# Turning u by a transposing transfer instead of TensorE and ScalarE, with a schedule of nine sets of ranks, in a fused threshold-attention and mixer kernel

## The chip, the cores and the metric

The kernel runs on one core of one Trainium2 chip. Its time is the device time of one execution in microseconds. The number quoted for the kernel before is the median of three runs. The profile is that of one further execution.

## What is computed

Eight batches of eight attention heads (sequence 576, head size 64) go through an attention that keeps only scores close to each row's largest one. The result, laid out as 576 rows of 512 channels for each batch, then goes through a mixer: a low-rank mixing along the sequence and a two-layer perceptron with a residual.

```python
# attention: batch, heads, seq, head_dim = 8, 8, 576, 64
scores = scale * np.matmul(q, k.transpose(0, 1, 3, 2))
thresh = np.max(scores, axis=-1, keepdims=True) - tau
scores = np.where(scores >= thresh, scores, -1000000000.0)
scores = scores - np.max(scores, axis=-1, keepdims=True)
attn = np.exp(scores)
attn = attn / (np.sum(attn, axis=-1, keepdims=True) + 1e-09)
x = np.matmul(attn, v)                    # then heads side by side: 8 x 576 x 512
# mixer: rank 32, d_model 512, hidden 2048
xt = x.transpose(0, 2, 1)
h = xt @ U @ V
u = x + h.transpose(0, 2, 1)
ch = np.maximum(u @ w_ch1, 0.0) @ w_ch2
out = u + ch
```

The first layer of the perceptron contracts over the 512 channels. TensorE contracts over the partitions, so the kernel needs u with the channels on the partitions, that is, u turned. That turning is what the change touches.

## The kernel before

The kernel works through 32 pairs of heads (four for each batch), and has its own small list scheduler. Each piece of work is a task with an engine, a cost, the tasks that it depends on, and a function that emits the instructions. The scheduler simulates the five engines with those costs, and emits the tasks in the order that it finds. Each engine then executes its instructions strictly in that fixed order. Where several tasks of one engine could start, a rank decides: the time at which the task became ready, plus an offset for its kind of task. The offsets stand in a table with one column for each phase of the program.

```python
OFF = {
    "copy_main": (-65.55, 4.27, -33.19), "copy_rest": (46.32, -22.93, -32.89), ...
    # ... one entry for each kind of task, three numbers each
}
def add(self, *args, **kw):
    t = Task(*args, **kw)
    t.off = self.OFF[t.fn.__name__][self.phase]
# ...
def rank(c):
    s, t = c
    if t.when is not None:
        due = t.when <= steps + (1.0 if t.kind == kind else 0.0)
        return (t.when - 1000.0 if due else t.when + 1000000.0, s)
    return (t.ready + t.off, s)
```

A matmul group of the perceptron carries a `when`, counted in score steps. It goes first once that many score steps have been emitted, and otherwise it takes the place that nothing else wants. There are 144 score steps in all; `DUE` holds the number for each batch.

```python
DUE = (218.25, 193.25, 202, 58.75, 370.75, 342.5, 322.25, 741.75)
# ...
if e == PE:
    n = free[0]
    while at[PE] + 0.45 < s and last[n] <= at[PE]:
        self.filler(n)               # a matmul on the identity that nothing reads
```

The softmax of one score step (128 rows of two heads), cut: TensorE makes scores in PSUM, VectorE takes them out with their minimum, ScalarE makes the exponential, VectorE selects. GpSimd doubles a part of the result, and SyncE's transposing transfer turns the weights.

```python
nc.tensor.matmul(pair_bank[j][part, c, 0:HC], a.tT[hs, 0, rows], a.tT[hs, 1, cs], ...)   # L449
nc.vector.tensor_scalar(out=s_sb, in0=pair_bank[x][:, :, 0:HC], ...)                     # L462
nc.scalar.activation(out=e_sb, in_=s_sb, func=ACT.Exp, ...)                              # L482
nc.vector.scalar_tensor_tensor(out=w_sb[:, 0:S], in0=s_sb, ..., in1=e_sb, ...)           # L489
nc.gpsimd.tensor_copy(out=w_sb[:, xs, S:640], in_=w_sb[:, xs, 512:S])                    # L507
nc.sync.dma_start_transpose(to, w_ring[...])                                             # L513
```

What follows for a head pair (cut): the product with the values (L588 to L596), the low-rank product (L653), its spread (L668), the sum u, its narrowing to bf16, and the turning of u.

```python
def sum_u(_):                                                        # VectorE, L675
    nc.vector.tensor_add(out=bt.x[:, :, pr.cols], in0=bank[...], in1=bt.x[:, :, pr.cols])

def narrow_u(_):                                                     # ScalarE, L682
    nc.scalar.copy(out=pr.ub, in_=bt.x[:, :, pr.cols])

ub = done["ub", p] = add(SCA, 0.57, narrow_u, [u, got("uT_", p - 2), got("ub", p - 1)])

def turn_u(t):                                                       # TensorE, L690
    ps = bank[t.got[0]][:, 0:256].bitcast(BF16)
    for i in range(4):
        nc.tensor.transpose(ps[:, i * P:(i + 1) * P], pr.ub[:, i, :], identb)

uT_ = done["uT_", p] = add(PE, 0.23, turn_u, deps, banks=1, kind="uT")

def copy_u(_):                                                       # ScalarE, L696
    nc.scalar.copy(out=bt.uT[:, pr.hp, :], in_=bank[uT_.got[0]][:, 0:256].bitcast(BF16))
```

The perceptron of a batch reads `bt.uT` in its first layer, ScalarE applies the relu (L750), the second layer follows, and VectorE adds u (L805).

```python
nc.tensor.matmul(bank[t.got[0]], W1b[:, dt, ft * P:(ft + 1) * P], bt.uT[:, dt, :], ...)  # L760, "up"
nc.tensor.matmul(ch, R2[:, ft, lo:lo + P], W2b[:, ft, :], ...)                           # L793, "down"
```

The 64 rows of each batch that are left over beyond 512 are gathered over two batches. They are turned on TensorE (L727) and go through the first layer at L776.

Of the kernel before, what the change touches and what calls it, by code (L numbers as in the profile page):

```python
# [8 lines left out]
P = 128  # L9
FP32 = mybir.dt.float32  # L10
BF16 = mybir.dt.bfloat16
# [11 lines left out]
NPAIR = H // 2  # L23
NP = B * NPAIR
SOFT = 4
EARLY = 8


W1_AT = (1, 4, 6, 9, 11, 14, 16, 19)
W2_AT = (20, 21, 23, 24, 25, 26, 28, 29)  # L30

DUE = (218.25, 193.25, 202, 58.75, 370.75, 342.5, 322.25, 741.75)

# [11 lines left out]
PE, VEC, SCA, POOL, SP = range(5)  # L45
# [19 lines left out]
class Order:  # L65
# [12 lines left out]


    OFF = {  # L80
        "copy_main": (-65.55, 4.27, -33.19), "copy_rest": (46.32, -22.93, -32.89), "copy_tt":
        (55.52, 75.97, 78.39), "copy_u": (-9.24, 32.51, 27.95), "copy_u4": (-33.7, -103.34, 12.57),
        "copy_w": (26.76, -36.81, 20.04), "down": (9.11, -38.52, 30.41), "exponential": (-75.1,
        348.03, 34.33), "finish": (-81.29, -4.31, -38.11), "first": (-55.84, 39.98, -12.2), "high":
        (318.07, 5.62, 10.21), "inverse": (-108.97, -22.9, -67.36), "join": (10.42, -3.6, 8.15),
        "load": (-8.71, 35.51, -42.16), "low": (12.45, 36.07, 40.66), "low_part": (-39.21, 135.95,
        -5.41), "low_rank": (-33.23, -18.24, 8.92), "make": (-24.27, 38.39, 1.66), "narrow": (-16.4,
        -76.48, 195.67), "narrow_u": (60.65, 3.75, -17.1), "narrow_u4": (-18.43, 20.09, 16.7),
        "norm": (-28.14, -232.63, 8.05), "product": (124.81, 96.76, 14.8), "relu": (108.49, 92.35,
        46.18), "rest": (63.06, -59.16, 27.83), "scores": (-50.96, -12.67, -95.71), "select":  # L90
        (118.77, 57.08, 91.87), "send": (-69.4, 60.79, -21.09), "spread": (48.74, -2.19, -63.39),
        "spread4": (79.29, 25.05, 4.44), "spread_v": (11.62, 75.45, 21.95), "sum_u": (-26.95,
        -36.59, 53.52), "sum_u4": (54.92, -47.81, 31.47), "sums": (-140.25, 32.72, -84.66),
        "threshold": (-37.93, 79.1, -43.59), "turn4": (71.1, 12.6, 27.31), "turn_main": (-113.51,
        69.4, 58.93), "turn_pe": (-18.8, -21.2, 34.54), "turn_rest": (15.16, 27.93, 15.36),
        "turn_u": (-21.99, 92.75, -1.81), "turn_w": (-17.93, -115.14, 3.52), "twin": (-84.09,
        -15.28, -93.69), "up": (-7.21, -32.4, -1.5), "values": (-8.3, -68.34, -10.67), "weigh":
        (28.1, 41.88, 60.36), "weights": (8.1, -7.95, 22.31),
    }

    def __init__(self, nbanks, filler):
# [5 lines left out]
        self.tasks.append(t)  # L107
        return t
# [90 lines left out]
def kernel(  # L199
# [12 lines left out]
    nc = tc.nc  # L212
# [10 lines left out]
    identb = consts.tile([P, P], BF16, name="identb")  # L223
# [59 lines left out]
    bank = [psum.tile([P, 512], FP32, name=f"bank{n}") for n in range(4)]  # L283
# [8 lines left out]
    order = Order(len(bank), fill)  # L292
    add = order.add

    done = {}

    def got(*key):
        return done.get(key)
# [72 lines left out]
            pairs.append(Pair(b, hp, batches[-1]))  # L371


    def prepare_tasks(p):
        pr = pairs[p]
        loads = load_tasks(p, pr)
        before = [got("S", p - 2, 3), got("S", p - 2, 4)]
        for x, (name, t0) in enumerate((("q", 0), ("k", 5))):
            def turn_main(t, t0=t0):
                for i in range(4):  # L380
                    nc.tensor.transpose(bank[t.got[0]][:, i * P:(i + 1) * P],  # L381
                                        pr.qkraw[:, t0 + i, :, :], ident)
# [24 lines left out]

        def high(_):
            nc.scalar.copy(out=pr.vh[:, :, :, 0, :],  # L409
                           in_=pr.vraw.rearrange("p j t d -> p t j d"))  # L410

        def low(_):

            raw = pr.vraw.rearrange("p j t d -> p t j d")
            for part, tiles_, h in ((slice(0, P), slice(0, 4), 1), (slice(HB, P), slice(4, 5), 0)):
                nc.gpsimd.tensor_tensor(out=pr.vh[part, tiles_, :, h, :], in0=raw[part, tiles_],  # L416
                                        in1=pr.vh[part, tiles_, :, 0, :], op=ALU.subtract)

        t = done["vhi", p] = add(SCA, 0.7, high,
                                 loads["v"] + [got("AV", p - 2, g) for g in range(3)] + [got("vhi", p - 1)])  # L420
        done["vlo", p] = add(POOL, 1.6, low, [t])
# [4 lines left out]
    gate = {}  # L426

    def score_tasks(p, i):


        pr = pairs[p]
        n = step[0]
# [5 lines left out]
        def scores(_):  # L438

            for c in range(2):  # L440
# [11 lines left out]
        deps = [got(name, p + a) for a in range(2 if i == 4 else 1)  # L452
                for name in ("qT", "kT", "qk4T")]
# [6 lines left out]
        for x in range(2):  # L460
# [6 lines left out]
            t = add(VEC, 0.69, weigh, [S_, got("w", tiles[0] + x - NS)])  # L467
# [12 lines left out]
        for x in range(2):  # L480
# [44 lines left out]
            if i < 4 and (x == 1 and p < EARLY and i >= 1 or p == NPAIR - 1 and i == 3):  # L525
                t = done["wT", tiles[0]] = add(PE, 0.28, turn_pe, [twin_] + free, banks=1,
                                               kind="wT")
# [18 lines left out]
        if i == 4:  # L546

            def sums(_):
# [3 lines left out]
                                        dma=0.1)  # L552


    def value_tasks(p):
        pr = pairs[p]
        bt = pr.batch

# [13 lines left out]
        for g, tiles_ in enumerate(((0, 1), (2, 3), (4,))):  # L572
            n = len(tiles_)
# [39 lines left out]
            if soft:  # L613
                def make(_, rows=rows, over_sum=over_sum, av=av, n=n):
# [5 lines left out]
                              frees=[av]))  # L620
# [14 lines left out]
            t = add(SCA, 0.36 if n == 2 else 0.28, low_part, [av] + opens)  # L635
            t = add(VEC, 0.35 if n == 2 else 0.22, join, [t], frees=[av])
# [46 lines left out]

        ub = done["ub", p] = add(SCA, 0.57, narrow_u, [u, got("uT_", p - 2), got("ub", p - 1)])

        def turn_u(t):

            ps = bank[t.got[0]][:, 0:256].bitcast(BF16)
            for i in range(4):
                nc.tensor.transpose(ps[:, i * P:(i + 1) * P], pr.ub[:, i, :], identb)  # L690

        deps = [ub] + (done.get(("p1", pr.b - 2), []) if pr.hp == 0 else [])
        uT_ = done["uT_", p] = add(PE, 0.23, turn_u, deps, banks=1, kind="uT")

        def copy_u(_):
            nc.scalar.copy(out=bt.uT[:, pr.hp, :], in_=bank[uT_.got[0]][:, 0:256].bitcast(BF16))  # L696

        done["uT", p] = add(SCA, 0.53, copy_u, [uT_, got("uT", p - 1)], frees=[uT_])


        if not last:
            return
# [1 line left out]
        def spread4(t):  # L704
# [4 lines left out]
                                    banks=1, kind="h")  # L709
# [29 lines left out]
    ov = out.rearrange("b (p t) m -> b p t m", p=HB)  # L739

    def mixer_tasks(b):
        bt = batches[b]

        due = DUE[b]
        uT = [done["uT", b * NPAIR + hp] for hp in range(NPAIR)]
# [11 lines left out]
        for ft in range(16):  # L757
            def up(t, ft=ft):
                for dt in range(4):
# [3 lines left out]
            t = add(PE, 0.862, up, uT + weights1 + done.get(("o", b - 2), []), banks=1, kind="p1",  # L763
                    when=due + 35.75 * ft / 16)
# [3 lines left out]
        if bt.odd:  # L768

            done["p1r", b] = []  # L770
            for g in range(4):
                def rest(t, g=g):
                    for n in range(4):
# [6 lines left out]
                t = add(PE, 0.9, rest, [done["uT4", b], got("o4", b - 2)] + weights1, banks=1,  # L780
                        kind="p1", when=due + 3.5 + 10.25 * g)
# [94 lines left out]

    weight_loads()
    for p in range(0, NP, 2):
        order.phase = 0 if p < NPAIR else 1 if p < NP - NPAIR else 2
        prepare_tasks(p)  # L880
        prepare_tasks(p + 1)
        for i in range(NT):
            score_tasks(p, i)
        for i in range(4):
            score_tasks(p + 1, i)
        value_tasks(p)
        value_tasks(p + 1)
        if (p + 1) % NPAIR == NPAIR - 1:
            mixer_tasks(p // NPAIR)
# [37 lines left out]
```

## Time and profile before

| what | value |
|---|---|
| time, median of three runs | 615.9 us (615.58 to 616.2) |
| span of the profiled execution | 612.9 us |
| granted TensorE clock | 0.999 of full speed |
| DMA traffic | 87.35 MB, mean 143 GB/s |
| the transposes of u on TensorE (L690) | 128 instructions, 219 ns each |
| the copies of the turned u on ScalarE (L696) | 32 instructions, 579 ns each |
| the transposing transfers of the weights (L513) | 143, median 4.5 us from issue to landing |

The profile gives each engine's busy time, and groups instructions by the kernel's line. A busy TensorE is not necessarily a TensorE at its peak, because matmuls overlap in its pipeline: the durations of neighbouring matmuls add up to more than the time that they took together. For that reason the distance between the starts of neighbouring matmuls is used here wherever TensorE's work is counted.

### The profile page before, as it was taken

Reading aid. Unit: us, or ns where it says so; the run is one execution under the profiler, and the core shown is the slowest. Engines: PE = TensorE matmul, PEld = TensorE weight load, DVE = VectorE, ACT = ScalarE, POOL = GpSimd, SP = SyncE. Lnnn points to the kernel's source line nnn. Section 1 sums busy time; section 2 is a strip of 40 time slices with the busy share of each in tenths; the row PEclk is TensorE's granted clock in tenths of the full one; section 3 lists DMA queues with packets and bytes.
Section 4 is the critical chain, followed back from the end, with each engine's and each line's share of the span. In section 5 each row is a group of like instructions: output and inputs, shape, how many; then the busy total and the mean of one; then the engine's idle time right before and its main releaser. Section 6 shows DMA issues by size and latency. Waiting matters only on the chain.

```text
span 612.9 us, 17317 instructions
## 1 busy us (share of the span) xinstructions
PE 600.8 (98%) x6339; PEld 346.1 (56%) x6339; DVE 521.0 (85%) x1399; ACT 478.3 (78%) x983; POOL 361.2 (59%) x596
## 2 busy tenths in 40 slices
PE   7999999999999999999999999999999999999997
PEld 4465655656556555655456655564656655555553
DVE  3999998899999899899976999999998899994201
ACT  4778899988898867997687966998789877984540
POOL 8787768687887656556535755676675732442000
PEclk9999999999999999999999999999999999999999
DMA  7699989987999699977994799889867896464203
GB/s 158 124 167 150 170 152 155 149 157 152 185 163 160 147 174 155 176 146 153 177 157 89 127 182 158 163 135 169 164 129 135 160 196 115 88 126 87 65 13 73
DMA packets 209716, 87.35 MB, mean 143 GB/s; under 512 B 187744, under 2 KB 199984, under 8 KB 209632
## 3 DMA queue, kind: packets, MB, share of 16 engines
q1 hardware_dynamic: 194624, 63.15, 61.2%
q0 software_dynamic: 14048, 22.76, 19.6%
q8 instruction: 50, 0.82, 0.6%
q10 hardware_dynamic: 960, 0.34, 0.2%
q14 instruction: 34, 0.28, 0.2%
HBM read 37.90 MB, written 9.44 MB: 77 GB/s over the span
## 4 chain that ended last, share of the span: by engine, by line
PE 73%; DVE 1%; issue 1%; ACT 0%; DVEq 0%
PE scores L449 19%; PE bank L793 18%; PE bank L760 16%; PE bank L592 9%; PE bank L381 3%; PE bank L776 2%; PE bank L653 1%; PE bank L588 1%; PE bank L668 1%; PE bank L690 1%; PE bank L394 1%; DVE w_ring L489 1%; DVE s_sb L462 0%; PE bank L705 0%; PE bank L727 0%
## 5 line engine op out<-in xcount | busy, mean ns | idle before, releaser
L489 DVE SCALAR_TENSOR_TENSOR w_ring<-s_sb,thr,e_sb 128x576 bf16<-128x576 f32 x288 | 240.0, 861 | 4.5 <-ACT e_sb L482 2.6
L482 ACT ACTIVATE e_sb<-s_sb,m 128x576 bf16<-128x576 f32 x288 | 216.4, 772 | 35.0 <-DVE s_sb L462 34.4
L462 DVE TENSOR_SCALAR_CACHE_REDUCE s_sb<-scores 128x576 f32<-128x576 f32 x288 | 206.6, 748 | 28.5 <-PE scores L449 27.3
L449 PE MATMUL scores<-qkT 64*64 64x288 f32 x2304 | 178.3, 415 | 1.3 <-DVE s_sb L462 1.3
L507 POOL COPY w_ring<-w_ring 128x128 bf16<-128x128 bf16 (+1 forms) x168 | 71.1, 430 | 121.2 <-DVE w_ring L489 87.2
L793 PE MATMUL bank<-W2b,R 128*128 128x512 bf16 x576 | 136.9, 379 | 0.0
L760 PE MATMUL bank<-uT,W1b 128*128 128x512 bf16 x512 | 123.0, 380 | 0.0
L449 PEld LDWEIGHTS scores<-qkT 64*64 64x64 f32 x2304 | 77.7, 132 | 71.5 <-DVE s_sb L462 15.9
L750 ACT ACTIVATE R<-bank 128x512 bf16<-128x512 f32 x144 | 83.0, 592 | 19.2 <-PE bank L760 13.6
L326 POOL DMA_DIRECT2D qkraw<-in_q_dram x125 | 82.1, 663 | 13.8 <-PE bank L381 7.5
L640 POOL TENSOR_TENSOR x<-x,rec 128x256 f32<-128x256 f32 (+1 forms) x84 | 57.4, 685 | 52.4 <-DVE x L633 41.3
L793 PEld LDWEIGHTS <-R 128*128 128x128 bf16 x576 | 53.3, 98 | 57.2 <-issue 5.7
L326 POOL DMA_DIRECT2D qkraw<-in_k_dram x125 | 81.2, 654 | 2.8 <-issue 2.0
L760 PEld LDWEIGHTS <-W1b 128*128 128x128 bf16 x512 | 45.9, 98 | 53.4 <-issue 10.1
L416 POOL TENSOR_TENSOR vh<-vraw_ring,vh 128x512 bf16<-128x512 f32 x64 | 58.5, 914 | 11.7 <-ACT vh L409 8.8
L592 PE MATMUL bank<-vh,wT_ring 128*128 128x128 bf16 x896 | 64.3, 219 | 0.0
L592 PEld LDWEIGHTS <-wT_ring 128*128 128x128 bf16 x896 | 55.5, 98 | 7.6 <-issue 4.4
L805 DVE TENSOR_TENSOR o<-bank,x 128x512 f32<-128x512 f32 x36 | 24.7, 687 | 38.2 <-issue 19.6
L588 PE MATMUL bank<-vh,wT_ring 128*128 128x64 bf16 x256 | 49.3, 193 | 0.3 <-POOL vh L416 0.3
L387 ACT COPY qkT<-bank 128x512 f32<-128x512 f32 x64 | 35.5, 586 | 12.2 <-PE bank L381 11.9
L475 ACT ACTIVATE thr<-m,tau_t 128x2 f32<-128x2 f32 x144 | 42.1, 292 | 3.6 <-DVE s_sb L462 2.9
L381 PE MATMUL bank<-ident,qkraw 128*128 128x128 f32 x256 | 35.6, 275 | 0.0
(72 smaller groups left out, 592.1 us busy)
## 6 DMA issues: line engine op xcount, KB each, us to landing
out_dram<-o SPq DMA_DIRECT2D x71, 128.0 KB, 2.7
vraw_ring<-in_v_dram SPq DMA_DIRECT2D x32, 160.0 KB, 4.0
qkraw<-in_k_dram POOLq DMA_DIRECT2D x63, 80.0 KB, 3.8
qkraw<-in_q_dram POOLq DMA_DIRECT2D x62, 80.0 KB, 4.3
vraw_ring<-in_v_dram SPq DMA_DIRECT2D x32, 128.0 KB, 4.0
qkraw<-in_q_dram POOLq DMA_DIRECT2D x63, 64.0 KB, 4.1
qkraw<-in_k_dram POOLq DMA_DIRECT2D x62, 64.0 KB, 3.9
W1b<-in_moe_w_ch_dram POOLq DMA_DIRECT2D x8, 256.0 KB, 5.3
```

Of the source, the lines that this page charges most:

```text
L326: queue.dma_start(pr.qkraw[part, to, j, :], src[:, j, of, :])
L416: nc.gpsimd.tensor_tensor(out=pr.vh[part, tiles_, :, h, :], in0=raw[part, tiles_], in1=pr.vh[part, tiles_, :, 0, :], op=ALU.subtract)
L449: nc.tensor.matmul(pair_bank[j][part, c, 0:HC], a.tT[hs, 0, rows], a.tT[hs, 1, cs], start=True, stop=True)
L462: nc.vector.tensor_scalar(out=s_sb.rearrange("p (a c) -> p a c", a=2), in0=pair_bank[x][:, :, 0:HC], scalar1=-scale, scalar2=None, op0=ALU ...
L482: nc.scalar.activation(out=e_sb, in_=s_sb, func=ACT.Exp, bias=m[:, x:x + 1], scale=-1.0)
L489: nc.vector.scalar_tensor_tensor(out=w_sb[:, 0:S], in0=s_sb, scalar=thr_[:, x:x + 1], in1=e_sb, op0=ALU.is_le, op1=ALU.mult, accum_out=pr. ...
L507: nc.gpsimd.tensor_copy(out=w_sb[:, xs, S:640], in_=w_sb[:, xs, 512:S])
L592: nc.tensor.matmul(av[:, 2 * a + j, :], w, pr.vh[:, kt, j, :, :], start=kt == 0, stop=False)
L640: nc.gpsimd.tensor_tensor(out=x, in0=x, in1=over_sum(part), op=ALU.mult)
L750: nc.scalar.activation(out=R2[:, fts, lo:hi], in_=bank[t.got[0]].rearrange("p (f c) -> p f c", c=hi - lo), func=ACT.Relu)
L760: nc.tensor.matmul(bank[t.got[0]], W1b[:, dt, ft * P:(ft + 1) * P], bt.uT[:, dt, :], start=(dt == 0), stop=(dt == 3))
L793: nc.tensor.matmul(ch, R2[:, ft, lo:lo + P], W2b[:, ft, :], start=(ft == 0), stop=(ft == 15))
```

## The change

The transposes of u for a head pair leave TensorE, and the copy out of PSUM leaves ScalarE. In their place SyncE issues one transposing transfer for each pair, from the bf16 buffer `ub` straight into `uT`. It is the kind of transfer that already turns the softmax weights. It takes no PSUM bank. The turning of the left-over rows stays on TensorE.

The scheduler's offsets now have nine columns instead of three, and the column is chosen by the number of the head pair. The offsets and the numbers of `DUE` are new throughout, so the order of instructions changes on every engine. The diff, with the table of offsets cut:

```diff
+PHASES = (1, 2, 3, 4, 5, 6, 8, 28)
 ...
-DUE = (218.25, 193.25, 202, 58.75, 370.75, 342.5, 322.25, 741.75)
+DUE = (138.5, 263.5, 186, 264, 363.75, 374.25, 608, 1335.75)
 ...
-        "copy_main": (-65.55, 4.27, -33.19), "copy_rest": (46.32, -22.93, -32.89), "copy_tt":
+        "copy_main": (-161.33, 15.21, 54.53, -14.94, 0, -44.81, 16.33, 19.69, 58.92),
+        "copy_rest": (-53.78, -76.06, 30.75, -11.44, 11.84, -58.71, 74.1, 98.84, -36.38),
 ... (all entries of the table, from three numbers to nine)
+    def phase(p):
+        order.phase = sum(p >= n for n in PHASES)
+
     def prepare_tasks(p):
+        phase(p)
 ... (the same call in score_tasks, value_tasks and mixer_tasks)
-        def turn_u(t):
-
-            ps = bank[t.got[0]][:, 0:256].bitcast(BF16)
-            for i in range(4):
-                nc.tensor.transpose(ps[:, i * P:(i + 1) * P], pr.ub[:, i, :], identb)
-
-        deps = [ub] + (done.get(("p1", pr.b - 2), []) if pr.hp == 0 else [])
-        uT_ = done["uT_", p] = add(PE, 0.23, turn_u, deps, banks=1, kind="uT")
-
-        def copy_u(_):
-            nc.scalar.copy(out=bt.uT[:, pr.hp, :], in_=bank[uT_.got[0]][:, 0:256].bitcast(BF16))
-
-        done["uT", p] = add(SCA, 0.53, copy_u, [uT_, got("uT", p - 1)], frees=[uT_])
-
+        def turn_u(_):
+            nc.sync.dma_start_transpose(
+                bt.uT[:, pr.hp, :].rearrange("p (t r) -> p t r", t=4),
+                pr.ub.rearrange("p t c -> p (t c)"))
+
+        done["uT_", p] = done["uT", p] = add(
+            SP, 1.3, turn_u, [ub] + (done.get(("p1", pr.b - 2), []) if pr.hp == 0 else []), dma=0.9)
 ...
     for p in range(0, NP, 2):
-        order.phase = 0 if p < NPAIR else 1 if p < NP - NPAIR else 2
         prepare_tasks(p)
```

More of the change, by code (lines that the diff above doesn't have):

```diff
@@ L80 @@
     OFF = {
-        "copy_main": (-65.55, 4.27, -33.19), "copy_rest": (46.32, -22.93, -32.89), "copy_tt":
[L82 to L97, printed above, removed]
@@ L98 @@
-        (28.1, 41.88, 60.36), "weights": (8.1, -7.95, 22.31),
+        "copy_main": (-161.33, 15.21, 54.53, -14.94, 0, -44.81, 16.33, 19.69, 58.92),
+        "copy_rest": (-53.78, -76.06, 30.75, -11.44, 11.84, -58.71, 74.1, 98.84, -36.38),
+        "copy_tt": (14.2, -123.37, -32.51, 26.45, 34.76, 51.76, 43.12, 24.45, -19.84),
+        "copy_u": (5.09, 7.85, -128.89, -21.94, -50.84, 88.52, 22.76, -24.83, -6.87),
+        "copy_u4": (-57.46, 17.33, 19.5, 14.59, 26.45, -49.29, 37.5, -81.74, 11.21),
@@ new lines @@
+        "copy_w": (10.93, 111.7, 46.71, -43.74, -26.98, 54.66, -64.37, 0.64, 16.22),
+        "down": (-41.39, -17.11, 3.57, 17.13, -47.92, -32.2, 13.25, 65.57, 27.73),
+        "exponential": (17.08, 63.63, 64.99, 17.91, 617.68, 77.15, 529.14, 570.21, 55.92),
+        "finish": (44.03, 27.71, -32.98, 138.74, -78.18, 9.73, -10.51, -34.05, 50.2),
+        "first": (-111.95, -6.6, 27.16, -34.26, -79.27, 189.56, -10.81, -32.6, 12.09),
+        "high": (6.74, -5.53, -39.35, -18.36, -62.19, -47.6, -45.78, -90.56, 54.42),
@@ new lines @@
+        "inverse": (42.17, 41.66, -3.8, 46.45, -41.52, 59.4, -310.36, 51.29, 38.36),
+        "join": (-82.56, 14.29, 45.06, 26.15, -159.56, 40.1, -2.94, -82.81, -43.77),
+        "load": (11.81, -30.69, 15.51, 46.49, 59.57, 45.46, 42.24, 50.15, 5.56),
+        "low": (-95.41, -116.81, 5.41, -8.01, 43.11, 46.08, 44, 49.48, 195.25),
+        "low_part": (-6.39, 102.93, -21.79, 66.7, -43.25, 29.71, -225.07, -130.79, 182.44),
+        "low_rank": (-85.63, 50.01, -23.06, -3.1, 218.14, 30.74, -21.57, -42.88, 55.01),
@@ new lines @@
+        "make": (40, -14.35, 39.85, 58.48, 73.39, 6.86, 40.71, 1.85, -12.56),
+        "narrow": (55.72, 17.47, -10.02, -52.97, 21.77, 62.1, 6.85, 54.17, 23.39),
+        "narrow_u": (-19.68, 7.08, 73.56, 82.17, -9.12, 6.79, -36.63, 70.12, 36.58),
+        "narrow_u4": (-6.11, -29.19, 10.91, -53.27, -21.99, -40.06, -26.58, -146.84, 45.72),
+        "norm": (-25.43, -59.45, 10.09, -36.3, -60.01, -59.5, -41.79, 17.54, 20.42),
+        "product": (-47.3, -17.97, 59.34, -114.74, 19.61, -13.04, -48.2, 43.25, 16.89),
@@ new lines @@
+        "relu": (21.94, -28.28, -29.78, -10.71, -93.97, -64.77, -70.55, 39.43, 36.99),
+        "rest": (-53.64, -37.89, 7.21, -20.68, -48.19, 33.03, 15.29, -6.63, -54.66),
+        "scores": (-18.5, 143.77, -71.08, -51.69, -15.95, -2.27, 106.07, -44.2, -87.74),
+        "select": (-1.08, 85.42, 163.27, 201.94, 233.57, 232.87, 184.19, 267.74, -58.1),
+        "send": (-21.73, 28.24, -2.93, -28.49, 5.19, -29.46, 15.23, 39.26, -7.57),
+        "spread": (48.31, -72.08, -25.47, 9.72, 32.71, -81.6, 73.08, 92.45, -30.91),
@@ new lines @@
+        "spread4": (-13.7, 5.13, -43.42, 14.93, 61.29, -2.42, 163.5, -64.57, -74.88),
+        "spread_v": (64.99, 38.2, 34.59, -20.04, 23.5, 34.7, -38.34, -13.22, 85.24),
+        "sum_u": (-4.69, -130.58, -71.23, -45.95, -36.33, 31.04, 40.75, 114.47, -125.49),
+        "sum_u4": (-53.15, 7.68, 37.59, 58.34, 24.85, -71.54, -1.96, 7.5, -55.99),
+        "sums": (59.46, -33.38, 67.97, -34.41, 4.28, -18, 376.94, 138.68, -32.64),
+        "threshold": (11.69, -0.44, 82.26, 8.46, 24.73, 7.65, -311.39, -51.51, 15.76),
@@ new lines @@
+        "turn4": (19.54, 27.79, 39.73, -5.79, -164.35, 0.64, -9.59, -24.79, -67.53),
+        "turn_main": (-44.36, 37.82, -24.02, 26.95, 9.47, 30.49, 60.47, 160.95, -8.48),
+        "turn_pe": (15.05, -58.05, -28.69, 52.7, 39.97, -1.41, 115.73, 24.78, -13.99),
+        "turn_rest": (31.56, 34.87, -32.33, 91.55, 13.44, -26.54, -24.07, 10.67, 24.73),
+        "turn_u": (85.26, -11.66, -44.53, 41.31, -2.89, -12.42, -29.91, -11.1, 15.19),
+        "turn_w": (-29.3, 124.11, -117.11, 50.54, -16.97, -14.35, -86.23, -30.62, -23.09),
@@ L99 @@
+        "twin": (-108.65, -1.8, -17.67, -27, -2.62, 5.94, -35.16, -2.76, -2.33),
+        "up": (-44.55, 24.17, -52.48, 51.74, 24.32, -2.66, -26.4, 10.64, -52.95),
+        "values": (82.48, 5.58, -84.1, -51.12, -87.89, -16.54, 58.6, 374.53, -31.51),
+        "weigh": (-31.16, -39.6, 0.16, -108.62, -97.76, -0.96, -223.14, -33.74, 78.96),
+        "weights": (-114.79, -40.3, -53.48, -40.86, 17.94, 36.25, -54.13, 27.61, -7.02),
     }
@@ L428, in score_tasks @@
     def score_tasks(p, i):
+        phase(p)
         pr = pairs[p]
@@ L555, in value_tasks @@
     def value_tasks(p):
+        phase(p)
         pr = pairs[p]
@@ L741, in mixer_tasks @@
     def mixer_tasks(b):
+        phase(NPAIR * b + NPAIR - 1)
         bt = batches[b]
```

## The prediction

> **What bounds the kernel now.** I read four views, in this order: the page's busy times and chain, the same busy times cut into stages, the lists of waits, and the groups of the lines that the change touches.
>
> From the page, the busy time of each engine and the shares of the chain that ended last:
>
> ```profile
> PE 600.8 (98%) x6339; PEld 346.1 (56%) x6339; DVE 521.0 (85%) x1399; ACT 478.3 (78%) x983; POOL 361.2 (59%) x596
> ...
> PE 73%; DVE 1%; issue 1%; ACT 0%; DVEq 0%
> ```
>
> TensorE is busy nearly throughout and carries the chain. VectorE follows with 85%, and ScalarE is third. The stages say where that holds. I cut the span at score steps 0, 18 and 36 (their matmuls start at 9.5, 65.5 and 133.5 us), at 210 us, and at the end of the last score step (550.5 us). Columns: the stretch and its length, then busy us and instructions for TensorE, its weight loads, VectorE, ScalarE and GpSimd, then granted clock, DMA share and GB/s.
>
> ```profile
> 9.50:65.50 56.00, 53.59 (x702) 31.75 (x702) 52.42 (x149) 44.77 (x88) 43.61 (x76) 1.00 0.90 152
> 65.50:133.50 68.00, 67.30 (x795) 40.63 (x795) 63.02 (x173) 63.18 (x130) 51.33 (x88) 1.00 1.01 152
> 133.50:210.00 76.50, 75.40 (x859) 46.01 (x858) 73.50 (x191) 67.14 (x143) 61.35 (x98) 1.00 0.93 166
> 210.00:550.50 340.50, 340.50 (x3581) 194.32 (x3580) 314.58 (x847) 278.62 (x580) 193.24 (x314) 1.00 0.84 149
> 550.50:612.90 62.40, 57.81 (x383) 30.53 (x383) 15.25 (x31) 21.87 (x42) 3.87 (x8) 0.99 0.28 59
> ```
>
> From 210 us on TensorE has no idle time. At the beginning VectorE sets the pace: it is busy for 52.4 of 56 us, and TensorE is kept busy there with fillers, because no perceptron work exists before the first batch's u. At the end only perceptron work is left, on TensorE alone.
>
> Busy time overstates TensorE's work, so I measured each matmul from its start to the next start. The usual spacing is 216 ns for the 512-column products (L760, L793), 56 ns for 128 columns of bf16 (L690, L776, L592), 109 ns for the fp32 transposes (L381), and 1.13 us for the 16 matmuls of a score step. At those spacings the useful work of 144 score steps, 1,088 wide products and all the rest is 558 us. The 78 fillers took 20.6 us, and spacing above the usual another 26 us. Of these 26, only 0.7 to 1.0 us fall into each 30 us after 210 us. The loss sits at the start: 9.7 us before 90 us, 6.4 us from 90 to 210. TensorE starts at 3.3 us and ends 4.6 us before the span does. 558 + 20.6 + 26.2 + 3.3 + 4.6 is 612.7, the span.
>
> The waits of TensorE and SyncE (waiter, releaser: us in total, times, longest):
>
> ```profile
> PEld scores L449 <- DVE s_sb L462: 15.9, 39, 0.9
> ...
> PE bank L596 <- DMA wT_ring<-w_ring: 0.7, 1, 0.7
> ...
> SPq L513 <- POOL w_ring L507: 123.4, 71, 9.4
> ```
>
> TensorE waits for a transfer hardly at all. SyncE waits for its next weights far more than its transfers are waited for, so its queue usually has room.
>
> The lines that go, and the one that stays ahead of them:
>
> ```profile
> L682 ACT CAST ub<-x 128x512 bf16<-128x512 f32 x32 | 19.7, 615 | 7.9 <-DVE x L675 7.4
> L696 ACT COPY uT<-bank 128x512 bf16<-128x512 bf16 x32 | 18.5, 579 | 5.0 <-PE bank L690 4.8
> L690 PE MATMUL bank<-identb,ub 128*128 128x128 bf16 x128 | 12.5, 220 | 0.2 <-ACT ub L682 0.2
> ```
>
> L690 is 12.5 us of busy time, but 7.7 us from start to start, with 0.5 us of that above the usual spacing. Only the 7.7 us are time.
>
> [...] a 128-column transpose lasts 220 ns, and the next starts after 56. [...] All 143 of this kernel are bf16 from SyncE, and the 32 new ones join that stream. [...] The trace's DMA share of 1.01 between 65 and 133 us is what could make that matter.
>
> **The change part by part.** *Removed from TensorE:* 128 transposes and the spacing around them, 7.7 us, nearly all where TensorE is saturated (104 of the 128 start between 90 and 555 us). Worth 7.7 us at most.
>
> *Removed from ScalarE:* 32 copies of 579 ns, 18.5 us. ScalarE is at 78% and few waits end on it, so this lies beside other work: 0.
>
> *Added to SyncE and DMA:* 32 issues at about the 1.36 us that the weights' transposes take, 44 us on a queue that mostly waits. A weights' transfer of 128x1280 moves 1,280 packets of 256 bytes at 26.9 ns, 2.15 us of all 16 engines. One of 128x512 has 512 packets, an estimated 0.86 us. Thirty-two make 27.5 us, and the mean DMA share goes from 0.82 to about 0.86. Beside other work: 0, if nothing queues.
>
> *Latency:* TensorE and ScalarE needed about a microsecond to turn u. The transfer needs about 4.5 us. From the last spread of a batch to its first `up` that makes roughly 0.7 + 0.6 + 4.5 and some signals, 6.5 us. The new order allows for it. Counted in TensorE work at the spacings above, 8.6 us stand between these two in the first batch (2.3 before), and 9.7 us or more in all others (5.0 in the last one before). The price is that the first `up` now stands at score step 26 instead of 23, and ten more fillers (88 instead of 78) stand in the first 26 steps. Ten times 0.216 to 0.26 us is 2.2 to 2.6 us lost.
>
> *The new ranks:* the number of changes between score matmuls and others stays 288, so the loss there stays. What changes is the balance. Before, batch 3's `up` came due at step 58.75, and a run of 40 of them kept VectorE waiting: TensorE's work for steps 81 to 90 is 41.4 us where 32 to 33 is usual. With the new numbers only the first groups of batch 0 could come due before the end, and they are long done by then, so score steps go first and perceptron work fills gaps. The work after the last score step grows by 32 wide products net (6.9 us). It is moved, not added.
>
> *The sum.* By TensorE's whole sequence: -7.7 + 2.4 = -5.3 us. As a second way, I take step 27 as a common mark, which VectorE paces in both kernels (its work before it is the same). TensorE's work after it is 492.6 us before and 489.6 after, -3.0 us. The two differ because work removed from the VectorE-paced start brings nothing. Between them lies -4.2. I allow another -0.7 for a better-packed 90 to 210 us, where 6.4 us are lost against 3.8 at the later rate. 615.9 - 4.9 is **611.0 us**.
>
> **The rivals.** *VectorE becomes the bound.* Between steps 36 and 126 TensorE's work falls from 336.7 to 317.4 us without its usual 3% of loss. VectorE's, at its back-to-back spacings (678 and 740 ns for L462 and L489), is some 313 us. With 3% on both they are within a few per cent, and a TensorE in fixed order would stall on scores. For it: 15.9 us of waits already end on L462. Against it: from 270 to 300 us VectorE idles for only 1.7 us, and TensorE still loses only 0.9. If it happens I expect 3 to 8 us back, 614 to 619 us.
>
> *The transfer comes late.* In-order SyncE may hold a weights' transfer behind a u that isn't ready, or the first batch's u may land after its 8.6 us of cover: landing ranges from 3.0 to 8.6 us in this trace, and the DMA engines are full around 90 us. A stall of 2 to 4 us in the start, and small ones later: 613 to 616 us. Against it stands the single wait of 0.7 us on such a transfer among 143.
>
> *The schedule gains more than the transposes.* Tuned offsets could take out part of the 9.7 us of early loss. Against it: VectorE paces that stage, and the fillers rise rather than fall. With 4 us more: 607 us.
>
> **Range and chances.** The removable part is 7.7 us plus a few of scheduling, and the two main risks cost 2 to 8. So 605 to 617.5 should hold it 8 times in 10. Faster by over 2% means below 603.6 us, which needs the whole 7.7 and 4.6 more with no price paid: 0.06. Slower by over 2% means above 628.2, which needs both risks at twice their size: 0.03. Within 2%: 0.91.
>
> **What would show it.** L690 and L696 gone, and 32 transposing transfers into uT, landing after 4 to 5 us, with no TensorE wait on them beyond 1 us. TensorE busy without a gap from about 110 us. ScalarE's busy time down to about 460 us. The last score step ending some 10 us earlier, near 540 us. If TensorE instead shows growing waits on L462's successor after 130 us, the balance rival holds. If it waits on uT's transfer near 100 us, the latency rival does. A time below 605 would mean that spacing above the usual or fillers shrank beyond what the order shows.

## The result, and the profile after

The changed kernel takes 624.15 us (median of four, 622.9 to 625.95), against 616.05 us for the kernel before: a ratio of 1.0131 (95% interval 1.0099 to 1.0162). A second set of six on another chip gave 622.09 us (618.91 to 626.87) and 1.0078 (1.0038 to 1.0117). It is slower by about 1%. The prediction said 611.0, with a range up to 617.5.

The exchange itself took place as written. The tile view of uT in the changed kernel (count, then min/median/max ns of an issue, and us from issue to landing):

```profile
L722 SPq DMA_TRANSPOSE uT<-ub x32: 1188/1232/2177, 54.8 to 577.2; - x32
...
DMA to landing us min/median/max: 2.4/3.9/8.1
```

No TensorE instruction waits for one of these 32 transfers. The transposes and the copies are gone: ScalarE's busy time falls from 478.3 to 462.8 us. The page of the changed kernel:

```profile
PE 605.8 (97%) x6221; PEld 345.6 (55%) x6221; DVE 525.2 (84%) x1399; ACT 462.8 (74%) x951; POOL 358.8 (57%) x596
...
PE 84%; DVE 5%; DMA 4%; issue 3%; POOL 2%; ACT 1%; DVEq 0%; POOLq 0%; ACTq 0%
```

TensorE does less work, and yet it is busy 5 us longer and the span is 11 us longer. This chain covers the whole span. The one of the kernel before adds up to 75% only, since it reaches back no further than 150 us, so the 4% of DMA and the 5% of VectorE can't be set against it. The stages, cut at the same score steps as before (first score, steps 18 and 36, end of the last score):

```profile
10.30:75.20 64.90, 57.48 (x699) 34.12 (x698) 53.60 (x149) 44.45 (x87) 43.17 (x76) 0.94 1.02 140
75.20:145.90 70.70, 69.41 (x798) 41.30 (x797) 63.98 (x173) 60.33 (x122) 54.60 (x90) 0.99 0.93 146
145.90:556.30 410.40, 408.63 (x4322) 234.55 (x4320) 391.44 (x1040) 328.79 (x691) 251.03 (x410) 1.00 1.00 163
556.30:624.20 67.90, 63.31 (x391) 32.25 (x387) 13.97 (x28) 26.54 (x48) 2.22 (x5) 0.99 0.23 50
```

The lengths beside each other, with a second profiled execution of the same kernel:

| stage, us | before | changed | changed, another execution |
|---|---|---|---|
| until the first score step | 9.5 | 10.3 | 9.9 |
| score steps 0 to 18 | 56.0 | 64.9 | 59.5 |
| score steps 18 to 36 | 68.0 | 70.7 | 70.8 |
| step 36 to the last score's end | 417.0 | 410.4 | 409.1 |
| from there to the end | 62.4 | 67.9 | 67.8 |
| span | 612.9 | 624.2 | 617.1 |

The start is late: step 36 comes 12.4 us later than before in one execution and 6.7 us in the other. From step 36 to TensorE's end it is only 1.1 or 2.4 us shorter (474.8 us before, 473.7 and 472.4 after), although TensorE's work behind step 36, at the usual spacings, is 5.8 us less.

The same in terms of TensorE's time, worked out from start-to-start spacings as in the prediction. Useful work fell from 558 to 551 us, as foreseen. Fillers rose from 20.6 to 23.3 us, also as foreseen. The spacing above the usual rose from 26.2 to 41.9 us, and to 34.5 in the other execution. That is the term that the prediction left nearly unchanged.

Its largest pieces stand in the start: of the 15.7 us more, some 11 lie before step 36. TensorE's largest waits for transfers before, then in the changed kernel:

```profile
PE bank L596 <- DMA wT_ring<-w_ring: 0.7, 1, 0.7
PE bank L394 <- DMA qkraw<-in_k_dram: 0.6, 1, 0.6
```

```profile
PE bank L427 <- DMA qkraw<-in_k_dram: 3.8, 1, 3.8
...
PE bank L414 <- DMA qkraw<-in_k_dram: 3.0, 1, 3.0
```

L427 and L414 are the transposes of q and k. GpSimd issued the last load of k for pair 2 at 28.3 us, and it landed at 35.4. TensorE was ready for it at 31.8. In the kernel before, the last load of k for pair 2 was issued at 13.4 and landed at 15.8, and TensorE's transposes of that pair began at 21.6. The first of these waits comes before any transfer of u has been issued (54.8 us).

The timeline of TensorE there (start, us, line and tile, then the wait before it):

```profile
30.27 1.53 PE L483 MATMUL scores<-qkT 64*64 64x288 f32 x16
35.55 0.30 PE L427 MATMUL bank<-ident,qkraw 128*128 128x128 f32 x1 [3.75 <-DMA qkraw<-in_k_dram]
```

And the stretches of 1 us behind it (the sixth entry after the length, just behind the busy times, is the granted TensorE clock):

```profile
35.00:36.00 1.00, 0.45 (x12) 0.47 (x13) 0.00 (x0) 0.11 (x1) 0.00 (x0) 1.00 1.06 183
36.00:37.00 1.00, 1.00 (x26) 1.00 (x22) 0.00 (x0) 1.00 (x4) 0.00 (x0) 0.52 1.38 323
...
39.00:40.00 1.00, 1.00 (x17) 0.33 (x9) 0.51 (x2) 0.03 (x1) 1.00 (x3) 0.77 0.00 0
40.00:41.00 1.00, 1.00 (x32) 0.88 (x29) 0.89 (x3) 0.01 (x1) 0.49 (x1) 1.00 0.07 12
```

After the wait TensorE's granted clock was 0.50 for 3.4 us. Around the end of the second wait it was 0.50 from 70.2 to 77.0 us.

So I had three theories to tell apart. The load theory: the new ranks bring the loads of k too late in the first 80 us. The traffic theory: 32 more transfers slow all others down. The balance theory: with less work on TensorE, VectorE sets the pace, and the removed work comes back as waits.

### The profile page after: what moved, and what is told of

Its sections match the earlier page's. It is cut to its first block, busy times and chain, and to the rows that moved or that the text cites. A ratio compares the mean times of both kernels' runs of the same rounds, so it can differ in the third digit from the quotient of the medians.

```text
span 624.2 us, 17091 instructions
## 1 busy us (share of the span) xinstructions
PE 605.8 (97%) x6221; PEld 345.6 (55%) x6221; DVE 525.2 (84%) x1399; ACT 462.8 (74%) x951; POOL 358.8 (57%) x596
## 4 chain that ended last, share of the span: by engine, by line
PE 84%; DVE 5%; DMA 4%; issue 3%; POOL 2%; ACT 1%; DVEq 0%; POOLq 0%; ACTq 0%
PE scores L483 22%; PE bank L822 20%; PE bank L789 17%; PE bank L627 10%; PE bank L414 4%; DMA qkraw<-in_k_dram 2%; DVE w_ring L523 2%; DVE s_sb L496 2%; PE bank L805 2%; PE bank L318 2%; DMA wT<-w_ring 1%; PE bank L688 1%; PE bank L623 1%; PE bank L703 1%; PE bank L631 1%
## 5 line engine op out<-in xcount | busy, mean ns | idle before, releaser
L523 DVE SCALAR_TENSOR_TENSOR w_ring<-s_sb,thr,e_sb 128x576 bf16<-128x576 f32 x288 | 245.1, 877 | 6.7 <-ACT thr L509 3.5
L516 ACT ACTIVATE e_sb<-s_sb,m 128x576 bf16<-128x576 f32 x288 | 218.7, 771 | 36.3 <-DVE s_sb L496 35.3
L483 PE MATMUL scores<-qkT 64*64 64x288 f32 x2304 | 184.0, 418 | 1.6 <-DVE s_sb L496 1.5
L541 POOL COPY w_ring<-w_ring 128x128 bf16<-128x128 bf16 (+1 forms) x168 | 66.5, 401 | 163.2 <-DVE w_ring L523 109.3
L483 PEld LDWEIGHTS scores<-qkT 64*64 64x64 f32 x2304 | 81.0, 133 | 75.1 <-DVE s_sb L496 18.3
L789 PEld LDWEIGHTS <-W1b 128*128 128x128 bf16 x512 | 46.4, 98 | 54.9 <-issue 10.5
L675 POOL TENSOR_TENSOR x<-x,rec 128x256 f32<-128x256 f32 (+1 forms) x84 | 56.1, 669 | 27.7 <-DVE x L668 18.7
L449 POOL TENSOR_TENSOR vh<-vraw_ring,vh 128x512 bf16<-128x512 f32 x64 | 62.6, 978 | 5.3 <-ACT vh L442 2.4
L414 PE MATMUL bank<-ident,qkraw 128*128 128x128 f32 x256 | 37.9, 284 | 3.5 <-DMA qkraw<-in_k_dram 3.0
```

The lines of the kernel that those rows point to most:

```text
L414: nc.tensor.transpose(bank[t.got[0]][:, i * P:(i + 1) * P], pr.qkraw[:, t0 + i, :, :], ident)
L516: nc.scalar.activation(out=e_sb, in_=s_sb, func=ACT.Exp, bias=m[:, x:x + 1], scale=-1.0)
L523: nc.vector.scalar_tensor_tensor(out=w_sb[:, 0:S], in0=s_sb, scalar=thr_[:, x:x + 1], in1=e_sb, op0=ALU.is_le, op1=ALU.mult, accum_out=pr. ...
```

## The experiments

### The two parts of the change, each alone

**Only the exchange.** The kernel before, with its three sets of ranks and its DUE:

```diff
-        uT_ = done["uT_", p] = add(PE, 0.23, turn_u, deps, banks=1, kind="uT")
-        ... (transposes and copy_u)
+        done["uT_", p] = done["uT", p] = add(SP, 1.3, turn_u, [ub] + ..., dma=0.9)
```

> The kernel before with one part of the change: u is turned by the transposing transfer, the three sets of ranks and DUE stay as they were (the scheduler still lays out the work anew; 103 fillers, first up at score step 27). The load theory (the new ranks bring k's loads too late in the first 80 us) expects no k-load wait over 1 us and a time near the kernel before, 613 to 621 us, with the fillers as its price. The traffic theory (32 more transfers slow all loads and keep the gain away) expects a time like the changed kernel's, 622 us or more, with loads of k landing after 5 us or more in the median. The balance theory (VectorE too close to TensorE once the transposes are gone) expects the loss after 150 us to grow as in the changed kernel, by some 5 us.

Measured: 628.42 us, ratio 1.0201 (1.0156 to 1.0245). No wait for k is over 1.3 us, and the landing time of qkraw's loads between 100 and 500 us is 4.2 us in the median against 4.1 before. It is slower than the changed kernel, which none of the theories had. The scheduler laid out everything anew for the changed task, with old offsets: fillers take 25.6 us instead of 20.6, and between 360 and 390 us the spacing above the usual is 8 us instead of 0.9, with waits of 0.8 to 1.0 us of L653, L698, L381 and L394 on ScalarE and VectorE. Step 36 comes at 135.6 us, near the 133.5 of before. So the late start belongs to the new ranks, and the old ranks lose elsewhere.

**Only the ranks.** The changed kernel with u on TensorE and ScalarE again.

> The changed kernel with the other part alone: the nine sets of ranks and the new DUE, but u turned on TensorE and copied by ScalarE again (85 fillers, first up at score step 24). The load theory expects waits for k's loads of some us in the first 80 us again, and 622 to 630 us, since the 7.7 us of transposes are back as well. The traffic theory expects a time near the kernel before, 615 to 619 us, with landing times like its own.

Measured: 632.65 us, ratio 1.0256 (1.0223 to 1.0289), with waits for k of 2.0 and 0.6 us. It is slower than expected by either theory. The new ranks and the new DUE together cost time with no transfer of u at all; the two were not separated. Step 36 came at 139.9 us, and the rest to TensorE's end took 486.9 us, 12 us more than before. With the exchange, with which they came, these ranks lose less (624.15).

### Is it the transfers' traffic?

The changed kernel in its own order, the transfers left out, uT zeroed once (so the first layer works on zeros):

```diff
         def turn_u(_):
-            nc.sync.dma_start_transpose(...)
+            pass
```

> The changed kernel with its order of instructions on every engine, but the 32 transposing transfers of u left out (uT is set to zero once at the start, so the first layer works on zeros). This takes away the transfers' traffic, their place in SyncE's queue and every wait on them. The load theory expects 621 to 624 us, with the two waits for k's loads near 32 and 68 us still there: the first of them comes before any transfer of u. The traffic theory expects 608 to 614 us, landing times back at the kernel before's 3.9 us for k, and no wait near 68 us.

Measured: 623.78 us, ratio 1.0119 (1.0089 to 1.0148). Taking all 32 transfers away is worth 0.4 us, and the zeroing delays the first filler by 2.2 us (the first score step by 0.8), so a few us at most. Of the two waits for k that the load theory expected, only the second is there, near 68 us. In place of the first stands a later one for the softmax weights:

```profile
PE bank L633 <- DMA wT<-w_ring: 3.5, 1, 3.5
PE bank L416 <- DMA qkraw<-in_k_dram: 2.2, 1, 2.2
```

From step 36 to the end of TensorE's work it is 473.7 us with the transfers and 473.8 without. The loads of q and k between 100 and 500 us landed after 4.1 us in the median before, 4.9 in the changed kernel, and still 4.7 without the transfers. The traffic theory falls.

### Is it the late loads of k?

**All eight loads of a pair together**, pairs 2 to 7:

```diff
+                if 2 <= p < 8 and kind == "k":
+                    return
                 queue.dma_start(pr.qkraw[part, to, j, :], src[:, j, of, :])
+                # ... behind the fourth load of q: the four loads of k
```

> The changed kernel with one thing moved: for head pairs 2 to 7, GpSimd issues the four loads of k directly behind the four loads of q, instead of where the ranks put them. TensorE, VectorE, ScalarE and SyncE keep their order. The load theory expects the two waits (3.8 and 3.0 us) and the lower granted clock behind them to go, and 611 to 616 us. The traffic theory expects the engines' queues to be just as full and the time to stay within 3 us of the changed kernel's 624.

Measured: 628.56 us, ratio 1.0208 (1.0178 to 1.0238): slower still. TensorE's waits in this run:

```profile
PE bank L563 <- POOL w_ring L550: 7.2, 4, 3.6
PE bank L640 <- DMA wT<-w_ring: 4.5, 2, 4.0
```

The waits for k are gone (0.3 us in all), and 11.7 us of others stand in their place: GpSimd, which starts its work in the order emitted (in the profiles before and after, all 590 of its transfers, copies and sums did), now makes its copies of the softmax weights (L550) late, with the loads ahead of them. My edit moved the shortage to another place.

**A gentler edit**: only pairs 2 and 4, and only to where the first of the four loads of k stood. Run twice, the second time beside the changed kernel on one chip.

```diff
+                if p in (2, 4) and kind == "k":
+                    # at the first of the four: issue all four; at the others: nothing
```

> The changed kernel in its order, with one edit on GpSimd: for head pairs 2 and 4 all four loads of k are issued where the first of them stood (21 us instead of up to 28, and 60 instead of up to 64). It delays the copies behind them by 2 and 1.3 us. If the start's lateness comes from these two waits (6.8 us) and the half clock after them, they go, step 36 comes near 138 us instead of 146, and the time is 613 to 618 us. If the start is short of transfers or of GpSimd in general, another wait takes their place and the time stays within 3 us of 624.

> The changed kernel once more, beside the next run on the same chip: 622 to 626 us.

> The changed kernel with the loads of k of head pairs 2 and 4 grouped, once more, since its runs scattered from 616.1 to 622.6 us. If the two waits for k count towards the end, 3 to 6 us less than the changed kernel in the same call; if other waits take their place in full, within 1.5 us of it.

Measured: 622.04 us (616.11 to 622.56) the first time, 621.22 us (617.35 to 622.69) the second, ratios 1.0056 (1.0005 to 1.0106) and 1.0052 (1.0018 to 1.0087). The changed kernel beside it took 622.09, ratio 1.0078 (1.0038 to 1.0117). That is 0.9 us less in the median, within the scatter: waits of 2.7 us or less on transfers (wT, q, k) stand in their place, about 6 us in all in either profile. So the two waits are not what makes the kernel slow in general. Where they are long, a single execution is slower. In the changed kernel's other profiled execution the same two waits are shorter:

```profile
PE bank L427 <- DMA qkraw<-in_k_dram: 1.9, 2, 1.7
...
PE bank L414 <- DMA qkraw<-in_k_dram: 0.9, 1, 0.9
```

Its granted clock stays at 1.00 in the first two stages, step 36 comes 5.7 us earlier, and it took 618.91 us against 625.95. The ten times of this kernel spread over 8 us. That this scatter comes from how landings fall is suggested by these two profiles, and not shown for the other eight.

**The clock.** Fillers ahead of the two transposes that wait, so that TensorE doesn't idle there:

```diff
         def turn_rest(t):
+            if p == 2:
+                for _ in range(16):
+                    fill(t.got[0])
 ... (13 in the same way ahead of pair 4's transpose of k)
```

> The changed kernel in its order, with 16 fillers ahead of the transpose of pair 2 and 13 ahead of that of pair 4 that wait for k near 32 and 68 us, so that TensorE does not idle there. The waits for k stay. If the half granted clock after each of these waits (0.50 for 3.5 and 7 us) is part of the loss, 617 to 621 us; if only the waits themselves count, within 1.5 us of the changed kernel's 624.

Measured: 623.25 us, ratio 1.0112 (1.0089 to 1.0135). The clock no longer drops (0.998 over the span), and the time is within 1 us of the changed kernel's. But in this profile the two last loads of k landed at 33.3 and 68.4 us, and the fillers ran until 35.2 and 69.7. They held TensorE some 2 and 1 us longer than the loads did, so this run doesn't tell what the half clock costs. In the changed kernel's two profiles it goes together with the long waits, and the two aren't told apart.

**Old ranks for the start only.**

> The changed kernel with the old ranks for the first eight head pairs (the old first column for pairs 0 to 3, the old second column for pairs 4 to 7), the new ranks and the new DUE for the rest (99 fillers, first up at score step 27). If the loss sits in the new ranks of the start, score step 36 comes at 134 to 137 us instead of 145.9, and the time is 612 to 618 us. If any ranks that were not found for exactly this program lose some 10 us, it is 620 us or more.

Measured: 625.23 us, ratio 1.0165 (1.0117 to 1.0212), scattered from 620.57 to 628.88. Its profile is of the fastest of these. Step 36 came there at 136.0 us, as expected of it, so the late start does belong to the new ranks there. But the rest took 478.2 us to the end of TensorE's work, 4.5 us more than in the changed kernel: a different start gives the scheduler a different rest. The time is in the range of the second theory, 620 us or more.

### What is an order worth, without any exchange?

The kernel before, u on TensorE, the same work, only the switch from the first to the second set of ranks two pairs later:

```diff
-        order.phase = 0 if p < NPAIR else 1 if p < NP - NPAIR else 2
+        order.phase = 0 if p < NPAIR + 2 else 1 if p < NP - NPAIR else 2
```

> The kernel before with all its work and u on TensorE; only the switch from the first set of ranks to the second comes two head pairs later (6 instead of 4). The work is the same, the order another (98 fillers, first up at step 26). If the ranks before were found for exactly this order and any other loses, 622 us or more, without any exchange. If orders of this scheduler lie close together, 614 to 619 us.

Measured: 626.4 us, ratio 1.0161 (1.0128 to 1.0194). 10.5 us are lost by nothing but another order, and the time lies in the first of the two ranges expected. TensorE's fillers, first before, then in this run:

```profile
L289 PE MATMUL bank<-identb 128*128 128x512 bf16 x78 | 22.2, 408 | 3.3 <-DVE identb L224 3.3
```

```profile
L289 PE MATMUL bank<-identb 128*128 128x512 bf16 x98 | 27.3, 408 | 3.3 <-DVE identb L224 3.3
```

Twenty more fillers are 5 us busy, and step 36 comes at 141.8 us instead of 133.5. No single wait is over 1.1 us beyond the one at the very beginning. Such lateness has no one culprit in the list of waits.

### What is the exchange worth in a fixed order?

These runs keep the order of before on all engines and change only what the turning tasks emit.

**The turning left out** altogether (uT zeroed once, the first layer works on zeros), and, in a later run, only from the third batch on (24 of 32 pairs, stale values in uT, the start untouched):

> The kernel before in its own order of instructions, with the turning of u left out: no transposes on TensorE, no copies on ScalarE, no transfers (uT is set to zero once at the start, so the first layer works on zeros). It measures what taking this work away is worth when nothing else moves. If TensorE's order is the bound as the prediction had it, all 7.7 us come off: 607 to 610 us. If VectorE or the start's pace hold the end, at most half of it: 612 us or more.

> The kernel before in its own order, with the transposes and copies of u left out from the third batch on (24 of 32 head pairs; uT keeps the rows of batches 0 and 1, so the first layer works on stale values). The start is untouched. If TensorE's work is the bound from 150 us on, its 24 x 0.24 = 5.8 us come off: 609 to 611 us. If about half returns as waits for VectorE, as the run with all of them left out says from score step 36 on: 612.5 to 614 us.

Measured: 614.19 us, ratio 0.9961 (0.9937 to 0.9985), for the first. Its zeroing made the first score step come 2.9 us late, so it understates. The second: 612.55 us, ratio 0.9931 (0.9893 to 0.9968), 4.6 us less than before, of 5.8 us of work taken away. In the trace of the second, from step 36 to the last score's end:

```profile
135.60:549.40 413.80, 412.28 (x4350) 236.58 (x4350) 385.74 (x1036) 334.82 (x700) 253.81 (x410) 1.00 0.84 153
```

That is 413.8 us against 417.0, and 3.5 us less from step 36 to TensorE's end, so some 2 of the 5.8 us came back. TensorE's weight loads for the scores wait 13.5 us on VectorE's L462 in that stretch, instead of 11.7. The balance theory is right in kind, and about a third of the work in size.

**The turning moved** to the transfer, at the same place in the order:

```diff
-            nc.tensor.transpose(ps[:, i * P:(i + 1) * P], pr.ub[:, i, :], identb)
+            nc.sync.dma_start_transpose(bt.uT[:, pr.hp, :]..., pr.ub...)
```

> The kernel before in its own order, with the transposes and copies of u replaced by the transposing transfer, issued by SyncE at the place in the order where TensorE turned u. GpSimd's and VectorE's order is the same, TensorE's and ScalarE's lacks only the transposes and copies. The schedule theory (the exchange is harmless, the new order of everything costs the time) expects 609 to 616 us: 7.7 us off, and a few us of waits where the first up follows the last u closely (2.3 us of TensorE work in the first batch, 5.0 to 5.4 in three others, against some 6.5 us of path). The exchange theory (transfers cost more than the transposes) expects 620 us or more.

Measured: 636.07 us, ratio 1.0322 (1.0245 to 1.04). TensorE's largest wait, and the first place where it falls:

```profile
PE bank L760 <- DMA uT<-ub: 12.6, 3, 5.0
```

```profile
84.15 0.81 PE L760 MATMUL bank<-uT,W1b 128*128 128x512 bf16 x3 [0.36 <-ACT wT_ring L530]
89.74 0.58 PE L760 MATMUL bank<-uT,W1b 128*128 128x512 bf16 x1 [4.79 <-DMA uT<-ub]
```

Three times an `up` stands so close behind the last u of its batch that the transfer's latency shows, 12.6 us in all, and the granted clock is 0.50 around the end of each wait, for 17 us in all. By the spacings, these three places cost 18 us more than before, of 25 us more in the whole profile. The time is in the range of the exchange theory, but by the waits and the clock behind them. I had the place right and the size too small. So the whole exchange can't stay in the old order: it needs another, and another order has its price.

**Only where there is room.** The first three pairs of each batch by transfer, the fourth on TensorE:

> The kernel before in its own order, with u of the first three head pairs of each batch turned by the transposing transfer and that of the fourth still on TensorE and ScalarE. Only the fourth has its first up close behind. The schedule theory expects no wait on a transfer of u, TensorE's work lower by 24 x 0.23 = 5.5 us, about half of which comes back as waits: 612 to 615 us, faster than both kernels. The exchange theory expects 617 us or more from the traffic and SyncE's queue.

> The same, but from the third batch on the transfers of these three pairs are left out altogether (uT then keeps older rows there, so the first layer works on stale values). The difference to the run with them is what 18 transfers cost in traffic and in SyncE's queue. Schedule theory: within 1 us of it. Exchange theory: 3 us faster or more.

Measured: 617.61 us, ratio 1.0012 (0.9985 to 1.0039), with the transfers, and 615.55 us, ratio 0.9987 (0.9959 to 1.0014), with 18 of them left out. No TensorE wait on a transfer of u. The 24 transfers cost what the removed transposes bring, and 18 of them cost about 2 us of it (2.1 in the medians of six). The first time is just in the exchange theory's range, and the cost of the 18 lies between the two. With the 18 left out, TensorE turns u for 24 pairs fewer, as many as in the run above that gained 4.6 us, and here the gain is 0.4. Which of the two is nearer to the worth of that work stays open. None of the versions run here beats both kernels while it computes everything.

## Why the prediction was wrong

- **"Removed from TensorE: 7.7 us at most."** The mechanism was right as far as the runs go, the size off. In a fixed order, 24 of the 32 pairs are worth 4.6 us of their 5.8 (0.9931, 0.9893 to 0.9968), and in the run with six transfers left 0.4.
- **"Latency."** The path of the transfer was judged well: 3.9 us to land in the median, and no TensorE wait on it. The price in fillers was right too: 2.7 us for ten, 2.4 predicted.
- **"Added to SyncE and DMA: 0."** Nearly right. Leaving all transfers out of the changed kernel brings 0.4 us, and 18 of them in the old order 2 us. The DMA share rose from 0.82 to 0.90 where 0.86 was estimated; without the transfers it is 0.85.
- **"The new ranks" and "The sum."** This is the step that failed. I took the loss above the usual spacing, 26.2 us, as it was, and even allowed 0.7 us less, though every instruction stood in a new place. It rose to 41.9 us (34.5 in the other execution). That alone turns the -4.9 us of the sum into the +11 of this profile, and into most of the +4 of the other. The runs show in its place that the loss belongs to the order: the new ranks without the exchange cost 17 us, one phase switch moved by two pairs costs 10.5 us with the same work, and each of the five other orders from the scheduler, the changed kernel's among them, is slower than the one before.
- **"I take step 27 as a common mark, which VectorE paces in both kernels."** It came at 99.2 us before, and at 108.2 (102.3) after. VectorE was busy for 93.6% of score steps 0 to 18 before, and for 82.6% (89.3%) after. In the old start TensorE waited 0.6 us for k in all, and I read VectorE's pace there as a property of the stage, not of the order. The chain that I took as TensorE's showed nothing of this: it reaches back to 150 us only.
- **The rivals.** VectorE's balance was real but small. It is busy for 95.4% of the long third stage instead of 93.1% (388.1 of 417 us before, 391.4 of 410.4 after). The lateness of u's transfer did not occur in the changed kernel. The transfers that TensorE did wait for in the start were k's loads and the weights', whose issue times the new order had moved, and taking the long waits for k away brought no more than 0.9 us. I had looked at where fillers and `up` stand on TensorE, and not at where GpSimd's loads stand against their first use.

What stays open: why the start is 6.7 us late even in the better execution. Fillers are 3 us of it. The rest is spread over waits of 1 to 2 us on several transfers, and they changed places whenever I removed one. That the offsets of the kernel before had been found by trying on a chip, and those of the changed one less well, would explain that all other orders lose, but it was not tested here. Nor were the new offsets and the new DUE told apart.

## What to carry to other kernels

Where a change re-orders every engine, the losses of the old trace are those of the old order and can't be carried over. Price the order by itself, with a run that changes the order and not the work. An operation saved on the bound engine brought time here only in an order that stood, and swapping it for a longer path moved the order. With engines that start their work in the order emitted, as GpSimd did here, compare for each transfer of the new order its issue with its first use: pair 2's last load of k stood 8 us ahead of its pair's transposes before, and 3.5 us ahead of its use in the changed kernel, where it took 7.1 us in one profile and 5.0 in another.

## What was unexpected of the hardware

TensorE's granted clock fell from 1.00 to 0.50 around some of its waits, for 3.4 us or for twice that: for 3.4 us after the wait of 3.75 us that ended at 35.6 us, for 6.8 us around the end of the one of 3.0 us that ended at 71.2, and for 6.8 us around each of those of 4.8 and 5.0 us in the run with u moved. Shorter waits went both ways. In the run of the ranks alone, 2.00 us were followed by 0.50 (first two lines). In the second run with k's loads grouped, 2.74 us were not (last two):

```profile
33.00 0.30 PE L427 MATMUL bank<-ident,qkraw 128*128 128x128 f32 x1 [2.00 <-DMA qkraw<-in_k_dram]
34.00:35.00 1.00, 1.00 (x15) 1.00 (x12) 0.33 (x1) 1.00 (x3) 0.00 (x0) 0.50 1.31 323
37.80 0.41 PE L639 MATMUL bank<-vh,wT 128*128 128x64 bf16 x8 [2.74 <-DMA wT<-w_ring]
38.00:39.00 1.00, 1.00 (x36) 0.93 (x32) 0.47 (x2) 0.42 (x1) 0.00 (x0) 1.00 1.40 208
```

In the traces before and after, the granted clock has two values, 1.00 and 0.50. Single waits of 2.0 and 3.0 us had a stretch at 0.50 beside them, and the one of 2.74 us had none, so the length of a wait alone doesn't decide it here.

The time from issue to landing of one and the same load differed by execution: the last load of k for pair 2 took 7.1 us in one profile of the changed kernel and 5.0 in the other, and made TensorE wait 3.75 and 1.69 us.
